# Linear attention with a cosine feed-forward layer: attention chunks of 128 steps split into two sub-chunks of 64 steps

## Chip, cores and metric

One core of one Trainium2 chip. The metric is the device time of one run in microseconds (us); lower is better. Engines: PE (TensorE, matmuls; PEld is its weight load), DVE (VectorE), ACT (ScalarE), POOL (GpSimd), SP (SyncE, which here only issues DMAs).

## The reference

4 batches, 8 heads, 768 steps, head size 48. All in float32.

```python
for t in range(S):                      # per batch and head; state is 48 x 48
    y[t]  = r[t] @ (state + outer(u * k[t], v[t]))
    state = w[t][:, None] * state + outer(k[t], v[t])
x = y as (4*768 tokens, 8*48 = 384)
h = x @ w_in                            # 384 -> 2048
out = (h * cos(h)) @ w_out              # 2048 -> 384
```

## The kernel before

**Attention.** Each batch's 768 steps are cut into 6 chunks of 128, so there are 24 chunks; two chunks (the same place of two batches) make a block, and there are 12 blocks. Blocks 0 and 6 hold first chunks (no state yet), blocks 5 and 11 last chunks (no state needed after). Heads come in 4 pairs, a pair's two heads at partitions 0 to 47 and 64 to 111. The steps of a chunk, by the letters of the plan:

- `decay` (L202): two scans on DVE make the running products of w inside the chunk and from its end; r is multiplied by the one (L220), k by the other (L221).
- `diag` (L223): the u-weighted diagonal, spread on POOL into the two score tiles `asb` (L239), one for each head of the pair.
- `t` (L264): 4 transposes of k on PE, copied to `kn`.
- `a` (L254): 8 score matmuls (4 pairs x 2 heads, 48 rows, 128 x 128 result); then two DVE copies under a mask (L261) put the scores above the diagonal into `asb`.
- `s` (L277), for a block: k-by-v products into `pst` (L286), added on DVE to the decayed state (L293).
- `o` (L306), for a block: own products, v by `asb`, 16 matmuls over 128 steps into two PSUM banks `py`.
- `d` (L246): the state times the whole chunk's decay, `dd`. `p` (L318), for a block: `dd` times r is added into `py` (L326), ACT copies both banks to `yf`, and DMAs spread `yf` into `xf` (L335 and L302): 6 DMAs for each chunk, half from SP, half from ACT.
- `x` (L337): `xf` is split in a high and a low part, `xT`.

An fp32 matmul leaves two records of PE in the trace, a transpose one.

**Feed-forward.** Each block of 256 tokens passes 8 units. `mm1` (L377 on, matmuls at L390) is 18 matmuls of 128 weights and 256 columns; the gate (L354 on: ACT, DVE, ACT, ACT, DVE, then the high part, then two POOL subtractions) makes h cos h; `mm2` (L396 on, matmuls at L404) is 12 matmuls with 384 columns, three units behind (`LAG`). So there are 96 of each.

**Order.** PE's order is written out by hand: `START` for the first blocks, while the weights are fetched and unpacked on ACT and DVE, and then `PLAN`, eight rows, one per unit of a block, each naming the attention steps that stand between `mm1` and `mm2` (the number after + is the chunk or block, counted from the running one). The other engines follow in the order that a scheduler gives from priorities; `tc.high_priority` moves an instruction forward in it. `NEEDS` and `att()` pull a step forward that another needs. `BUFS` has the buffers of each tile; `EARLY` and `LATER` say which engine does which step in the two phases. Attention uses three PSUM banks in turn (two while two blocks run side by side).

Of the kernel before, what the change touches and what calls it, by code (L numbers as in the profile page):

```python
# [44 lines left out]
EARLY = dict(rkt="v", cd="a", wsg="v", wadd="v", wm="a", whi0="a", whi1="a", ksh="a", gh="a", yf="a", xh="a", rzh0="p", rzh1="v", r3="v", k3="p", rk="v", ru="p", rf0="v", rf1="v", kn="a", dd="v", rd0="a", rd1="a", rz0="v", rz1="v", ks="v", g0="p", g1="p", x="v", wlo0="v", wlo1="v", qf="s", qt="s", qr="s", qv="s", qx0="s", qx1="s", qo="s")  # L45
LATER = dict(ksh="v", gh="v", yf="a", xh="v", rzh0="a", rzh1="a", r3="p", k3="v", rk="v", ru="v", rf0="v", rf1="v", kn="v", dd="p", rz0="v", rz1="v", ks="p", g0="p", g1="p", x="v", qf="s", qt="s", qr="s", qv="s", qx0="s", qx1="a", qo="s")
# [11 lines left out]
START = ["lv0 decay0 diag0 t0 load0 f load1 d0 a0 f f f diag1 w t1 decay2 o0 f w diag2 d1 load3 lv3 d2 diag3",  # L58
# [10 lines left out]
def rwkv_cos_ffn(ctx: ExitStack, tc: tile.TileContext, tr, tn, u, ut, wts, w, rkw, vst, us, xs, out):  # L69
# [44 lines left out]
    shrink = cst.tile([R, NP], F32, name="shrink")  # L114
# [66 lines left out]
    def att_load(j):  # L181
# [5 lines left out]
        a["r3"] = tt[:, 0:512].rearrange("p (a t) -> p a t", a=NP)  # L187
        a["k3"] = tt[:, 512:1024].rearrange("p (a t) -> p a t", a=NP)
# [54 lines left out]
    def rows(h):

        return slice(ROW * h, ROW * h + HD)

    def att_dstate(a):

        if a["c"] == 0:
            return  # L250
        a["dd"] = dd = buf("dd", [R, NP, HD], F32)
        E["dd"].tensor_tensor(out=dd, in0=states[a["b"]], in1=a["ee"][:, :, 0:1].to_broadcast([R, NP, HD]), op=ALU.mult)
# [424 lines left out]
```

## Time and profile before

| | |
|---|---|
| time, median of 3 runs | 577.27 us (576.62 to 577.53) |
| span of the profiled execution, first to last instruction | 575.5 us |
| PE busy | 526.2 us, 91% |
| PEld busy | 500.6 us, 87% |
| DVE busy | 422.8 us, 73% |
| ACT busy | 247.6 us, 43% |
| POOL busy | 239.4 us, 42% |
| in the chain that ended last: PE, DVE, DMA | 60%, 21%, 8% |

The profiled execution's span is 1.8 us under the median; no other time of that execution is given. Busy shares are averages over a start of about 157 us, in which weights are prepared, and a regular part after it.

### The profile page before, as it was taken

What the parts mean: (1) busy time and instruction counts of PE and PEld (TensorE: products, weight loads), DVE (VectorE), ACT (ScalarE), POOL (GpSimd) and SP (SyncE); (2) the same over time, 40 slices, a digit from 0 to 9 for tenths busy, and PEclk for the clock granted to TensorE, in tenths of its full rate; (3) what the DMA queues carried; (4) which work ended last, traced back from release to release, by engine and by line L of the source; (5) the groups of instructions that cost most, each with busy time, mean ns of one, the idle gap of its engine ahead of it and who ended that gap; (6) DMA issues with size and microseconds to landing.
All of it is one profiled execution on the core that took longest, in us unless ns stands there. A gap on an engine that the chain in (4) does not pass through costs nothing.

```text
span 575.5 us, 11251 instructions
## 1 busy us (share of the span) xinstructions
PE 526.2 (91%) x4444; PEld 500.6 (87%) x4444; DVE 422.8 (73%) x694; ACT 247.6 (43%) x420; POOL 239.4 (42%) x288
## 2 busy tenths in 40 slices
PE   2667699987999999999999999999999999999995
PEld 2556698986999999899999999999899999999994
DVE  6988999998886967856858857857858559835441
ACT  2336777673443442442442342342342534335441
POOL 2240437464534544532643634534534443323331
PEclk9998999998999999999999999999999999999998
DMA  8937583010526116026132025034033026210001
GB/s 231 271 114 255 181 281 110 2 56 27 159 104 168 40 35 188 12 59 177 49 115 71 4 94 142 1 105 130 1 108 100 1 100 223 91 29 1 28 1 33
DMA packets 22988, 56.12 MB, mean 98 GB/s; under 512 B 4240, under 2 KB 15120, under 8 KB 22928
## 3 DMA queue, kind: packets, MB, share of 16 engines
q1 hardware_dynamic: 20336, 53.55, 30.5%
q10 hardware_dynamic: 2592, 1.77, 1.2%
q8 instruction: 37, 0.61, 0.4%
q14 instruction: 23, 0.19, 0.1%
HBM read 45.87 MB, written 4.72 MB: 88 GB/s over the span
## 4 chain that ended last, share of the span: by engine, by line
PE 60%; DVE 21%; DMA 8%; issue 4%; ACT 4%; POOL 2%; ACTq 0%; SPq 0%; DVEq 0%; POOLq 0%
PE ph L390 26%; PE acc L404 24%; PE pa L259 3%; PE py L316 3%; DMA xf<-yf 3%; DMA tt<-tr 3%; DVE tt L216 2%; DVE h L172 2%; DVE ee L209 2%; DVE h L165 2%; DVE w L141 2%; PE py L326 2%; DVE rr L362 2%; DVE rr L359 1%; PE pst L286 1%
## 5 line engine op out<-in xcount | busy, mean ns | idle before, releaser
L141 POOL TENSOR_TENSOR gs<-rr,gs 128x256 fp32r<-128x256 f32 x192 | 162.8, 869 | 224.1 <-DVE gs L138 168.4
L390 PE MATMUL ph<-xT,w 128*128 128x256 f32 x1728 | 227.6, 287 | 13.5 <-DVE rr L362 4.9
L390 PEld LDWEIGHTS ph<-xT,w 128*128 128x128 f32 x1728 | 217.2, 192 | 18.9 <-issue 4.8
L404 PE MATMUL acc<-w,gs 128*128 128x384 f32 x1152 | 220.4, 339 | 4.1 <-DVE gs L138 2.8
L404 PEld LDWEIGHTS acc<-w,gs 128*128 128x128 f32 x1152 | 197.3, 189 | 9.7 <-DVE gs L138 4.0
L360 ACT ACTIVATE rr<-rr 128x512 f32<-128x512 f32 x96 | 60.7, 632 | 130.0 <-DVE rr L359 130.0
L358 ACT ACTIVATE rr<-ph 128x512 int32<-128x512 f32 x96 | 56.5, 588 | 114.3 <-PE ph L390 76.9
L362 DVE SCALAR_TENSOR_TENSOR rr<-rr,ph 128x512 f32<-128x512 f32 x96 | 65.5, 682 | 49.1 <-ACT rr L361 48.6
L359 DVE SCALAR_TENSOR_TENSOR rr<-rr,ph 128x512 f32<-128x512 int32 x96 | 65.2, 679 | 27.7 <-ACT rr L358 27.4
L361 ACT ACTIVATE rr<-rr 128x512 f32<-128x512 f32 x96 | 60.6, 631 | 2.4
L239 POOL TENSOR_SCALAR_AFFINE_SELECT asb<-cd 128x512 f32<-128x512 f32 x48 | 34.6, 743 | 33.3 <-PE py L316 17.5
L138 DVE CAST gs<-rr 128x512 fp32r<-128x512 f32 x80 | 37.6, 470 | 9.6 <-PE acc L404 9.2
L209 DVE TENSOR_TENSOR_SCAN ee<-tt,one_e 112x516 f32<-112x516 f32 x24 | 30.8, 1285 | 15.1 <-DMA tt<-tr 14.7
L220 POOL TENSOR_TENSOR tt<-tt 112x512 f32<-112x512 f32 x18 | 24.1, 1340 | 32.4 <-DVE tt L216 32.4
L259 PE MATMUL pa<-tt 48*128 48x128 f32 x384 | 32.6, 305 | 4.2 <-DVE tt L220 3.5
L259 PEld LDWEIGHTS pa<-tt 48*128 48x128 f32 x384 | 27.2, 204 | 10.4 <-issue 5.6
L261 DVE COPY_PREDICATED asb<-mask,pa 128x512 f32<-128x512 uint8 x48 | 33.5, 729 | 1.6 <-PE pa L259 1.6
L216 DVE TENSOR_TENSOR_SCAN tt<-tt,inj 112x516 f32<-112x516 f32 x24 | 33.1, 1378 | 0.1
L316 PE MATMUL py<-asb,v 128*64 128x128 f32 (+1 forms) x384 | 27.5, 302 | 2.1 <-DVE asb L261 2.1
L316 PEld LDWEIGHTS py<-asb,v 128*64 128x64 f32 (+1 forms) x384 | 23.8, 145 | 4.7 <-DVE asb L261 3.3
L138 ACT CAST w<-h 128x768 fp32r<-128x768 f32 x16 | 13.2, 828 | 23.4 <-DVE h L172 23.4
L227 PE MATMUL pc<-u_by_head,rkt 112*128 112x2 f32 x48 | 9.3, 316 | 13.3 <-DVE rkt L206 9.4
(68 smaller groups left out, 365.3 us busy)
## 6 DMA issues: line engine op xcount, KB each, us to landing
tt<-tr SPq DMA_DIRECT2D x24, 674.2 KB, 5.9
raw<-wts SPq DMA_DIRECT2D x16, 768.0 KB, 5.6
rk<-tn SPq DMA_DIRECT2D x18, 384.0 KB, 4.1
v<-tn SPq DMA_DIRECT2D x24, 192.0 KB, 4.5
out<-ob SPq DMA_DIRECT2D x24, 192.0 KB, 2.0
ww<-w SPq DMA_DIRECT2D x6, 768.0 KB, 4.3
xf<-yf SPq DMA_DIRECT2D x30, 72.0 KB, 2.4
xf<-yf ACTq DMA_DIRECT2D x18, 72.0 KB, 3.5
```

The lines of the kernel that those rows point to most:

```text
L138: (nc.scalar.copy if E[name] is nc.scalar else E[name].tensor_copy)(out=out, in_=in_)
L141: E[name].tensor_tensor(out=out, in0=full, in1=high.bitcast(F32), op=ALU.subtract)
L216: nc.vector.tensor_tensor_scan(out=wp[:, 0:W129], data0=wp[:, 0:W129], data1=inj.rearrange("p a t -> p (a t)"), initial=0.0, op0=ALU.mult, ...
L259: nc.tensor.matmul(out=pa[h][:, p], lhsT=a["k3"][rows(h), p], rhs=a["r3"][rows(h), p], start=True, stop=True)
L316: nc.tensor.matmul(out=py[SWAPPED[p]][ROW * o:ROW * o + m, n, p // 2], lhsT=a["v"][:, head_cols(p, h, m)], rhs=a["asb", h][:, p], start=n ...
L358: nc.scalar.activation(nn, ph, AF.Copy, scale=INV2PI / W_SCALE)
L359: nc.vector.scalar_tensor_tensor(out=rr, in0=nn, scalar=-2.0 * math.pi * W_SCALE, in1=ph, op0=ALU.mult, op1=ALU.add)
L360: nc.scalar.activation(rr, rr, AF.Sin, scale=0.5 / W_SCALE)
L361: nc.scalar.activation(rr, rr, AF.Square)
L362: nc.vector.scalar_tensor_tensor(out=rr, in0=rr, scalar=-0.5, in1=ph, op0=ALU.add, op1=ALU.mult)
L390: nc.tensor.matmul(out=ph[:, fi], lhsT=wgt[u * FU + fi][:, 0, a, kt * 128:(kt + 1) * 128], rhs=xT[:, b, kt], start=n == 0, stop=n == 3 * K ...
L404: nc.tensor.matmul(out=accs[i][j][:, :DM], lhsT=gs[:, a, fi, j * C:(j + 1) * C], rhs=wgt[u * FU + fi][:, 1, b], start=u == 0 and fi == 0 a ...
```

## The change

Each chunk is cut into two sub-chunks of 64 steps (q = 0, 1). The decay scans restart at each sub-chunk (8 instead of 4 stretches of the same total length). Scores, own products, state products and products with the past are made for each sub-chunk, with 64 rows or 64 columns, so that four matmuls address the four 64 x 64 quadrants of the array. The state is passed from the first sub-chunk to the second inside the block. Own products come in two visits, `o` and `b`, each with one sub-chunk of every pair; after each a small DVE copy (`settled`) reads the PSUM bank. Scores (`A`) and transposes (`T`) come once per block in the plan, no longer once per chunk. `xf` is one tile per block, and its DMAs are 6 per block. The diagonal tile is made by a POOL multiplication. `START`, `PLAN` and `PAIR` are new.

```diff
-BUFS = dict(... asb=4, ... kn=2, ee=2, dd=2, xf=6, ...)
+BUFS = dict(... asb=2, whole=6, sn=2, s0=2, ... kn=1, ee=2, dd=4, xf=2, ...)
-PLAN = ["t+2 t+3 mm1 mm2",
-        "a+2 mm2 mm1 decay+4",
-        "mm2 a+3 mm1 diag+4",
-        "mm1 o+1 mm2 diag+5 p+1 load+6 lv+6 load+7 lr+7 x+2",
-        "mm1 s+1 mm2 lv+7 x+3",
-        "mm1 mm2",
-        "mm1 mm2",
-        "mm1 d+4 d+5 mm2 decay+5 lr+6"]
+PLAN = ["T+1 mm2 mm1",
+        "mm1 A+1 mm2 decay+4",
+        "mm1 s+1 mm2 diag+4",
+        "mm1 o+1 mm2 decay+5",
+        "mm1 b+1 mm2 diag+5",
+        "p+1 mm1 mm2 load+6 lv+6 load+7 lr+7",
+        "mm2 mm1 x+2 lv+7",
+        "mm1 d+4 d+5 mm2 x+3 lr+6"]
...
+    def decayed(a, q, state):
+        w_all = a["whole"].rearrange("p (a q) -> p q a", q=2)[:, q].unsqueeze(2).to_broadcast([R, NP, HD])
+        a["dd", q] = dd = buf("dd", [R, NP, HD], F32)
+        (nc.vector if q and a["c"] == 0 else E["dd"]).tensor_tensor(out=dd, in0=state, in1=w_all, op=ALU.mult)
+    def att_scores(some):
...
+                for q in range(2):
+                    for h in range(2):
+                        nc.tensor.matmul(out=pa[h][subs(q), n, p], lhsT=a["k3"][rows(h), 2 * p + q],
+                                         rhs=a["r3"][rows(h), 2 * p + q], start=True, stop=True)
...
+                    nc.tensor.transpose(out=pt[h][:part * SUB, n, p, :HD], identity=ident[rows(h), rows(h)],
+                                        in_=a["k3"][rows(h), 2 * p:2 * p + part].rearrange("p q t -> p (q t)"))
...
+                    for q in range(2 if a["c"] < NCB - 1 else 1):
+                        nc.tensor.matmul(out=pst[q][ROW * h:ROW * h + m, n, p], lhsT=a["kn"][subs(q), n, head_cols(p, h, m)],
+                                         rhs=a["v"][subs(q), at:at + HD], start=True, stop=True)
...
+                    mid = buf("s0", [R, NP, HD], F32)
+                    nc.vector.tensor_tensor(out=mid, in0=pst[0][:R, n], in1=a["dd", 0], op=ALU.add)
+                decayed(a, 1, mid)
...
+    def att_own(i, second=0):
...
+            for pair in ((1, 0), (2, 3)) if second else ((0, 1), (3, 2)):
+                for p in pair:
+                    q = SWAPPED[p] ^ second
...
+                        nc.tensor.matmul(out=outs[i][SWAPPED[p]][ROW * o:ROW * o + m, n, p // 2, subs(q)],
+                                         lhsT=a["v"][subs(q), head_cols(p, h, m)], rhs=a["asb"][subs(q), h, n, p],
...
+        with tc.high_priority(offset=HP):
+            nc.vector.tensor_copy(out=settled[ROW:ROW + 1], in_=outs[i][SWAPPED[p]][ROW:ROW + 1, n, p // 2, subs(q)][:, 0:1])
...
+            for q in range(0 if a["c"] > 0 else 1, 2):
+                for p in (0, 1, 3, 2):
+                    for h in range(2):
+                        nc.tensor.matmul(out=py[SWAPPED[p]][rows(h ^ SWAPPED[p]), n, p // 2, subs(q)], lhsT=a["dd", q][rows(h), p],
+                                         rhs=a["r3"][rows(h), 2 * p + q], start=False, stop=True, skip_group_check=True)
```

## Rows read from the trace of the kernel before

**Rows 1.** The page: span, and busy time, share and instructions of each engine.

```profile
span 575.5 us, 11251 instructions
PE 526.2 (91%) x4444; PEld 500.6 (87%) x4444; DVE 422.8 (73%) x694; ACT 247.6 (43%) x420; POOL 239.4 (42%) x288
```

**Rows 2.** Busy time by stage: stretch, its length, busy time (and instructions) of PE, PEld, DVE, ACT, POOL, then the granted clock of PE, the DMA share and GB/s. The last one is one block of the plan.

```profile
0.00:40.00 40.00, 21.29 (x146) 18.80 (x148) 33.83 (x56) 13.74 (x22) 13.42 (x19) 1.00 0.74 195
40.00:80.00 40.00, 29.86 (x230) 27.72 (x228) 36.42 (x48) 25.75 (x40) 10.15 (x9) 0.91 0.70 237
80.00:120.00 40.00, 37.39 (x300) 35.43 (x298) 39.83 (x57) 29.61 (x49) 22.89 (x18) 1.00 0.28 88
120.00:157.00 37.00, 30.42 (x262) 28.09 (x262) 32.75 (x46) 17.85 (x32) 20.71 (x23) 0.95 0.29 84
157.00:290.34 133.34, 131.28 (x1149) 124.64 (x1147) 97.36 (x174) 50.93 (x90) 60.36 (x74) 1.00 0.31 93
417.47:459.11 41.64, 41.64 (x378) 40.07 (x377) 29.75 (x53) 16.07 (x30) 18.70 (x24) 1.00 0.24 72
```

**Rows 3.** The waits of PE from 157 us to the end: us in total, times, longest.

```profile
PE acc L404 <- DVE gs L138: 2.8, 5, 0.9
PE acc L404 <- POOL gs L141: 0.7, 2, 0.5
PE ph L390 <- DVE rr L362: 0.6, 1, 0.6
```

**Rows 4.** PE's timeline over one block of the plan (start in us, time to the modelled end of the last record, instruction, records). What a group costs is the distance from its start to the next one's.

```profile
417.47 1.16 PE L259 MATMUL pa<-tt 48*128 48x128 f32 x16
418.56 4.58 PE L390 MATMUL ph<-xT,w 128*128 128x256 f32 x36
423.07 1.96 PE L316 MATMUL py<-asb,v 128*64 128x128 f32 x32
424.96 2.36 PE L404 MATMUL acc<-w,gs 128*128 128x384 f32 x12
427.25 1.09 PE L326 MATMUL py<-tt,dd 48*48 48x128 f32 x32
428.27 1.13 PE L286 MATMUL pst<-v,kn 128*64 128x48 f32 x32
429.33 2.42 PE L390 MATMUL ph<-xT,w 128*128 128x256 f32 x18
431.59 2.25 PE L404 MATMUL acc<-w,gs 128*128 128x384 f32 x12
433.67 2.31 PE L390 MATMUL ph<-xT,w 128*128 128x256 f32 x18
435.82 2.25 PE L404 MATMUL acc<-w,gs 128*128 128x384 f32 x12
...
446.38 0.93 PE L268 MATMUL pt<-ident,tt 112*128 112x112 f32 x8
447.08 2.40 PE L390 MATMUL ph<-xT,w 128*128 128x256 f32 x18
...
459.11 1.16 PE L259 MATMUL pa<-tt 48*128 48x128 f32 x16
```

**Rows 5.** PE's timeline through one group of products with the past, cut at 341.66, 341.81 and 341.92 us (records started by then), and its last records.

```profile
341.63 0.33 PE L326 MATMUL py<-tt,dd 48*48 48x128 f32 x4
341.63 0.44 PE L326 MATMUL py<-tt,dd 48*48 48x128 f32 x8
341.63 0.55 PE L326 MATMUL py<-tt,dd 48*48 48x128 f32 x12
...
342.43 0.29 PE L326 MATMUL py<-tt,dd 48*48 48x128 f32 x4
```

**Rows 6.** Groups of instructions over the whole span, each shape apart: line, engine, operation, out<-in, shapes, count, then busy us and mean ns of one, then idle time before them.

```profile
L239 POOL TENSOR_SCALAR_AFFINE_SELECT asb<-cd 128x512 f32<-128x512 f32 x48 | 34.6, 743 | 33.3 <-PE py L316 17.5 <-ACT cd L138 8.9 <-DVE cd L235 6.1
L261 DVE COPY_PREDICATED asb<-mask,pa 128x512 f32<-128x512 uint8 x48 | 33.5, 729 | 1.6 <-PE pa L259 1.6
L220 POOL TENSOR_TENSOR tt<-tt 112x512 f32<-112x512 f32 x18 | 24.1, 1340 | 32.4 <-DVE tt L216 32.4
L252 POOL TENSOR_TENSOR dd<-sn,ee 112x192 f32<-112x192 f32 x16 | 7.9, 516 | 15.3 <-DVE sn L293 15.3
L138 DVE COPY kn<-pt 128x384 f32<-128x384 f32 x14 | 7.6, 549 | 0.7 <-PE pt L268 0.7
L293 DVE TENSOR_TENSOR sn<-pst,dd 112x192 f32<-112x192 f32 x16 | 4.9, 348 | 4.3 <-PE pst L286 4.3
L138 ACT COPY kn<-pt 128x384 f32<-128x384 f32 x6 | 2.8, 465 | 0.0
```

**Rows 7.** ACT's timeline after the past products of a block; ACTq is its queue issuing DMAs.

```profile
342.77 1.07 ACT L138 COPY yf<-py 112x512 f32<-112x512 f32 x2 [2.01 <-PE py L326]
343.87 0.53 ACTq L335 DMA_DIRECT2D xf<-yf  x1
...
350.37 0.60 ACT L358 ACTIVATE rr<-ph 128x512 int32<-128x512 f32 x1 [6.53 <-PE ph L390]
```

**Rows 8.** DVE's timeline in the block of rows 4: the last write of the next block's input, and a gate cast among its longest.

```profile
440.24 0.59 DVE L141 TENSOR_TENSOR xT<-xf,xT 128x384 fp32r<-128x384 f32 x1
...
446.30 1.05 DVE L138 CAST gs<-rr 128x512 fp32r<-128x512 f32 x1
```

More of the change, by code (lines that the diff above doesn't have):

```diff
@@ L243, in rows @@
[L243 to L252, printed above, removed]
-    def att_scores(a):
-        pa = [bank("a", [C, NP, C], "pa") for h in range(2)]
-        for p in range(NP):
-            for h in range(2):
-                nc.tensor.matmul(out=pa[h][:, p], lhsT=a["k3"][rows(h), p], rhs=a["r3"][rows(h), p], start=True, stop=True)
-        for h in range(2):
-            nc.vector.copy_predicated(a["asb", h], mask, pa[h])
@@ L263, in att_transpose @@
-    def att_transpose(a):
-        if a["c"] == NCB - 1:
-            return
-        pt = bank("a", [C, NP, 2, ROW], "pt")
-        for p in range(NP):
-            nc.tensor.transpose(out=pt[:, p].rearrange("t h d -> t (h d)")[:, :R], in_=a["k3"][:, p], identity=ident[:R, :R])
-        a["kn"] = kn = buf("kn", [C, DM], F32)
-        copy("kn", kn.rearrange("t (a h d) -> t a h d", h=2, d=HD), pt[:, :, :, :HD])
+        n = a["j"] % BLK
+        if n == 0:
+            a["asb"] = buf("asb", [C, 2, BLK, NP, SUB], F32)
+        else:
+            a["asb"] = atts[a["j"] - n]["asb"]
@@ new lines, in att_dstate @@
+    def att_dstate(a):
+        if a["c"] > 0:
+            decayed(a, 0, states[a["b"]])
+    def att_scores(some):
+        pa = [bank("a", [C, BLK, NP, SUB], "pa") for h in range(2)]
+        for a in some:
+            n = a["j"] % BLK
+            for p in range(NP):
+                for q in range(2):
+                    for h in range(2):
+                        nc.tensor.matmul(out=pa[h][subs(q), n, p], lhsT=a["k3"][rows(h), 2 * p + q],
+                                         rhs=a["r3"][rows(h), 2 * p + q], start=True, stop=True)
+        at = slice(some[0]["j"] % BLK, n + 1)
+        for h in range(2):
+            nc.vector.copy_predicated(some[0]["asb"][:, h, at], mask.unsqueeze(1).to_broadcast([C, len(some), NP, SUB]), pa[h][:, at])
@@ new lines, in att_transpose @@
+    def att_transpose(some):
+        pt = [bank("a", [C, BLK, NP, SUB], "pt") for h in range(2)]
+        part = 2 if some[0]["c"] < NCB - 1 else 1
+        for a in some:
+            n = a["j"] % BLK
+            a["kn"] = buf("kn", [C, BLK, DM], F32) if n == 0 else atts[a["j"] - n]["kn"]
+            for p in range(NP):
+                for h in range(2):
+                    nc.tensor.transpose(out=pt[h][:part * SUB, n, p, :HD], identity=ident[rows(h), rows(h)],
+                                        in_=a["k3"][rows(h), 2 * p:2 * p + part].rearrange("p q t -> p (q t)"))
+        at = slice(some[0]["j"] % BLK, n + 1)
+        kn = some[0]["kn"].rearrange("t n (a h d) -> t n a h d", h=2, d=HD)
+        for h in range(2):
+            copy("kn", kn[:part * SUB, at, :, h], pt[h][:part * SUB, at, :, :HD])
@@ L277, in att_state @@
     def att_state(i):
-        two = [a for a in (atts[i * BLK + n] for n in range(BLK)) if a["c"] < NCB - 1]
-        pst = bank("a", [C, BLK, NP, HD], "pst") if two else None
+        two = [atts[i * BLK + n] for n in range(BLK)]
+        pst = [bank("a", [C, BLK, NP, HD], "pst") for q in range(2)]
         for n, a in enumerate(two):
@@ L330, in att_past @@
         copy("yf", yf[:, :, 1:3], py[1][:R])
+        xf = buf("xf", [128, BLK, KT, C], F32)
         for n in range(BLK):
-            xf = atts[i * BLK + n]["xf"] = buf("xf", [128, KT, C], F32)
-            for h in range(2):
-                part = yf[rows(h), n]
-                E["qx%d" % h].dma_start(out=xf[h * HD:(h + 1) * HD], in_=part[:, 0:3])
-                spread(xf, part[:, 3], h)
+            atts[i * BLK + n]["xf"] = xf[:, n]
+        for h in range(2):
+            E["qx%d" % h].dma_start(out=xf[h * HD:(h + 1) * HD], in_=yf[rows(h), :, 0:3])
+            spread(xf, yf[rows(h), :, 3], h)
     def att_x(a):
@@ L437, in att @@
         for m in ("decay" if n == "diag" and j < BY_PE else NEEDS.get(n, "")).split():
-            for c in (range(j * BLK, (j + 1) * BLK) if whole and m not in "osp" else (j,)):
+            for c in (range(j * BLK, (j + 1) * BLK) if whole and m not in "obspTA" else (j,)):
                 att(c, m)
@@ L455, in att @@
             att_load(j)
+        elif n in "TA":
+            both = [j * BLK + m for m in range(BLK) if (j * BLK + m, n.lower()) not in seen]
+            seen.update((c, n.lower()) for c in both)
+            if both:
+                steps[n]([atts[c] for c in both])
         else:
```

139 lines of the change are left out of this document (72 added, 67 removed), and 8 rows, old and new, of the table START.

## The prediction

> **What bounds the kernel now.** First the page: PE is busy 91% of the span [rows 1]. A share says little over stages, so next the stages [rows 2]. Until 157 us PE idles 38 us (157 less 21.3, 29.9, 37.4 and 30.4), and DVE is busy 33.8, 36.4 and 39.8 of three times 40 us: that start is set by DVE's unpacking of weights and the chains around it. From 157 us on PE is the bound: 131.3 of 133.3 us, then 41.64 of 41.64 us in one block of the plan, with DVE at 29.8, POOL at 18.7 and ACT at 16.1. Third, PE's waits in that part [rows 3]: 4.1 us in all, 3.5 of them for gate outputs that DVE and POOL deliver late. So a microsecond less of PE work in a block is a microsecond of time, from 157 us on; before that it mostly is not.
>
> Fourth, what a block of PE consists of [rows 4]. One mm2 takes 2.08 us (431.59 to 433.67), one mm1 2.15; eight of each make 33.9. Attention groups: scores 1.09 twice, own products 1.89, past 1.02, state 1.06, transposes 0.70, together 6.85. The remaining 0.9 of 41.64 lies at the edges: mm2 after the own products takes 2.29 instead of 2.08, about 0.1 on entering and 0.1 on leaving a visit whose matmuls do not fill the array. Four such visits at 0.21 and a cheap one (the transposes) make 0.9. **Attention on PE is 7.8 us of a block.**
>
> **What a quadrant costs.** The past products already use four quadrants (48 rows, 48 columns). Their records start in fours: 4, 8 and 12 records by 341.66, 341.81 and 341.92, the last four at 342.43 [rows 5], so 8 quartets at 0.109 to 0.114 us; with 0.15 at the end that is 1.02 [rows 4]. I write a group as sets x cadence + 0.15. State: 16 pairs in 1.06, so 0.057 a pair, with 48 columns and weights 64 wide; scores: 8 pairs in 1.09, 0.117, with 128 and 128. The own products, 16 pairs of 128 columns in 1.89, give 0.109 again.
>
> After the change a set is four matmuls with 64 (or 48) columns and weights 48 to 64 wide. Bounds of its cadence: below, half the past's quartet, 0.055; above, the past's quartet unchanged, 0.109, if halving the columns buys nothing. I take 0.058, nearest the state row: it is the only row with weights 64 wide and few columns.
>
> PE, one block after: scores 64 records, 16 sets, 1.08; state the same, 1.08; past 64 records, 1.08; own products two visits of 8 sets, 0.61 each; transposes 16, in pairs over the rows, 8 sets, 0.61 if they go at the state's cadence (bounds 0.5, and 1.09 at the scores' cadence, whose weights are 128 wide too). Sum 5.07. Visits: T, A, s, o, b, p, six at 0.21, 1.26, since the past and state products no longer share one. Together 6.33 against 7.78: **1.45 less**.
>
> From 157 us on nine blocks remain (3 to 11). Six regular ones: -8.7. Block 6 has no past before (6.76) and half of one after (5.86): -0.9. Blocks 5 and 11 have neither transposes nor state products before (5.93) but half of both after (5.75): -0.2 each. **PE term: -10.0 us**.
>
> **The other engines.** DVE, per block: two mask copies of 512 go (2 x 729 ns), the kn copies move to ACT (2 x 549 ns), two more state additions come (2 x 348 ns) and two `settled` copies of one element at 0.2 us (no row has one; bounds nothing and the 348 ns of an addition): -1.5 us of 29.8 [rows 2, 6]. ACT gains two copies near 465 ns [rows 6], but after the past products it issues three DMAs for the block rather than six: today its next gate step starts at 350.37, 6.5 us after the copies at 342.77 to 343.84, behind those issues [rows 7]. I take 3 us of that as freed, half (bounds 0 and 6.5). SP's issues halve too, with the same bytes. POOL: four selects (743 ns) become two multiplications (1340 ns by the r product), two more `dd` (516 ns): +0.7 of 18.7, hidden by 22 us of idle time. With less on DVE and ACT the gate outputs come earlier; of the 4.1 us of waits [rows 3] I take half away: -2 (bounds 0 and -4.1).
>
> **New waits.** `settled` stands on DVE between an own visit and the next writer of `py`. `b` follows `o` after mm2 and mm1, 4.2 us; `p` follows `b` after a single mm2, 2.08 us. Ahead of `settled` DVE may be inside an operation of 1.05 us or so [rows 8] and then needs 0.2: covered once, not with two such in front. Behind it in DVE's order wait gate steps, three units (12.7 us) ahead of their mm2. I take one block in three losing 0.7: +2 to +3, taken as +2 (bounds 0, and 1.1 in each of 12 blocks, +13). The state chain (sum, second `dd` on POOL 0.52, past) has two visits, two mm2 and two mm1 before `p`: hidden.
>
> The next block's input: the past start at 427.25, the last write of xT ends at 440.83 [rows 8], its mm1 is at 447.08 [rows 4], 6.2 us to spare. After, `p` has only three mm1, four mm2 and T before that mm1, 16.8 us instead of 19.8; the 3 us from fewer DMA issues give it back. Loads of the next chunk move two rows later in the plan, still four rows (17 us) ahead of their scan. Both cost nothing while that cover lasts.
>
> **The start.** Three blocks of attention shrink there, 4.4 us of PE at most, half of which I count where PE is near its bound (37.4 of 40 us [rows 2]). DVE there changes by: 12 mask copies half as long (-2.8), four state additions (+1.4), six more `dd` (about 516 to 615 ns each on it, +3), `settled` (+1): near +2.5. The first block gains a chain (state, second `dd`, past) before its x. Net 0, bounds -6 and +5; this is the least certain term, since the whole order of the start is new.
>
> **Sum.** Against the profiled execution: 575.5 - 10 - 2 + 2 + 0 = 565.5 of span. The median stands 1.8 us above that span; I add it: **567.3 us**.
>
> **Rivals.**
> 1. *Halving the columns buys nothing*: sets keep 0.109, because what spaces the records is their issue and not their columns. For: no group of rows 4 has records closer than 0.027 us on average (past 0.87 us for 32); the changed kernel has some 1640 more of them. Against: within a quartet four records start inside 0.03 us [rows 5]. Then a block costs 3 x 1.89 + 2 x 1.02 + 0.61 + 1.26 = 9.58, +1.8; nine blocks +18: **595 us**. It decides from a cadence of 0.081 on, where 64 sets eat the gain.
>
> A rule on issue bears on this. The Trainium skill, "TensorE: Matmul & The Clock Gate", section "Wait — 56ns, not 53.3ns?", says that starts of matmuls never come closer than about 25 ns, however small they are. By that figure a set of four takes 0.100 us, a regular block 9.0 us, and the time would be about 591, an estimate. The quartets of [rows 5] break it between quadrants, but not as a mean over a group.
>
> 2. *`settled` eats the gain*: DVE, near 70% busy, has two operations ahead of it in most blocks and `p` waits about 1.1 us in each: 12 x 1.1 = 13 instead of 2: **578 us**. For: DVE is in order and late in these rows already [rows 3]. Against: it loses 1.5 us of work in a block, and the copy is moved forward by priority.
> 3. *Only pairs overlap*: the quadrants do not run four at a time when both halves of a chunk share rows. Cadence 0.058 for two, 10.1 a block: near 598 us. The past products speak against it.
> 4. *The start gains as well*: shorter first chains let the first mm1 begin earlier, -6, and the waits vanish, -4: **557 us**. For: PE idles 38 us there. Against: DVE, which fills that stage, does not get less work.
>
> **Chances.** The forecast, 560 to 572: 0.52. Rival 4: 0.13. Rival 2 with all that ends between 572 and 582: 0.18. Rivals 1 and 3: 0.17. The range 554 to 582 holds the first three but for tails, 0.8. A measurement of this kernel tells about 0.2% (1.2 us). Faster takes forecast, rival 4 and the lower half of rival 2's band: 0.74; within 0.2%: 0.05; slower 0.21.
>
> **What would show it.** Right: score, state and past groups of 64 records at 1.0 to 1.15 us, own visits near 0.6, a regular block near 40.2 us, PE records about 6080. Wrong: quartets near 0.1 us; waits of the past or second own products for DVE above 0.5 us per block; PE waiting for xT at a block's first mm1; or the last weight's unpacking, and with it the regular part, starting several us later than 157.

## The result and the profile after

The changed kernel takes 585.87 us (median; 582.12 to 586.86) against 577.4 for the kernel before in the same runs: ratio 1.0148, 95% interval 1.0106 to 1.0189. It is slower by 1.5%. The forecast was 567.3, range 554 to 582, faster; the time lies outside the range and on the other side. The profiled execution took 586.22 us, its span is 584.5. In the table of experiments a median is over all executions and a ratio over the undisturbed ones alone; of e2's four executions two were disturbed, the profiled one among them, so its marks stand in brackets.

The page after (answers to [rows 1]): PE has 11 us less work, and yet the span is 9.0 us longer. So PE idles 20 us more.

```profile
span 584.5 us, 14459 instructions
PE 514.9 (88%) x6084; PEld 489.4 (84%) x6084; DVE 415.9 (71%) x716; ACT 258.5 (44%) x445; POOL 241.7 (41%) x280
```

To divide those 9.0 us I use two marks: the start of the 17th mm1 (the third block's first, where the regular part begins) and of the 96th, the last. Before they stand at 157.4 and 557.6 us, after at 164.4 and 566.3. **Start +7.0, regular part 401.9 against 400.2, so +1.7, end +0.3.** The regular part was to lose 10.

Busy time by stage after, columns as in [rows 2]. In the last line, one block, PE idles 1.4 of 41.6 us (the stretch opens inside a wait of 2.40 us); the block of [rows 2] has no idle time.

```profile
0.00:40.00 40.00, 17.20 (x282) 14.98 (x285) 34.43 (x61) 14.17 (x24) 9.39 (x14) 1.00 0.72 233
40.00:80.00 40.00, 27.21 (x369) 24.33 (x367) 37.70 (x55) 23.49 (x36) 13.30 (x9) 0.87 0.62 188
120.00:164.00 44.00, 36.03 (x434) 32.52 (x434) 36.27 (x61) 16.95 (x32) 24.17 (x23) 0.92 0.28 83
417.00:458.60 41.60, 40.18 (x512) 38.59 (x512) 25.60 (x50) 16.87 (x30) 19.50 (x24) 1.00 0.23 63
```

The waits of PE from 168 us on (answers to [rows 3]; total, times, longest). The two waits for gate outputs of before (3.5 us) are nearly gone. In their place stands one that [rows 3] has at 0.6 us: mm1 waits until DVE has read a PSUM bank `ph` of an earlier mm1 (its last reader is L403). One more wait, 0.7 us for `xT`, lies between the first mark and 168 us: 14.1 us in all from mark to mark, 4.1 before.

```profile
PE ph L431 <- DVE rr L403: 11.1, 6, 2.4
PE pst L313 <- DVE asb L281: 1.3, 1, 1.3
PE py L348 <- DVE s L320: 0.6, 1, 0.6
PE acc L445 <- POOL gs L155: 0.4, 1, 0.4
```

PE's timeline over one block (answers to [rows 4]). Every group costs what was forecast: scores 294.39 to 295.48, 1.09; state 1.06 (of 32 records: half the others are missing); own products 0.62 twice; past 1.04; transposes 0.63. The loss is in the mm1 at 248.53 and 290.58, each the second of two mm1 that follow one another (row 0 of PLAN ends with mm1, row 1 begins with it): 1.76 and 1.88 us of idle time in front of them. The first takes 2.29 us, the second 3.81 (the last section shows its clock), and another one, at 460.60, takes 3.38, and the scores behind it 1.49 for 1.09.

```profile
248.53 2.36 PE L431 MATMUL ph<-xT,w 128*128 128x256 f32 x18 [1.76 <-DVE rr L403]
250.82 1.16 PE L277 MATMUL pa<-tt 48*64 48x64 f32 x64
...
256.31 1.13 PE L313 MATMUL pst<-v,kn 64*64 64x48 f32 x32
257.37 2.35 PE L445 MATMUL acc<-w,gs 128*128 128x384 f32 x12
...
261.76 0.69 PE L348 MATMUL py<-asb,v 64*64 64x64 f32 x32
262.38 2.35 PE L445 MATMUL acc<-w,gs 128*128 128x384 f32 x12
...
266.78 0.69 PE L348 MATMUL py<-asb,v 64*64 64x64 f32 x32
267.39 2.35 PE L445 MATMUL acc<-w,gs 128*128 128x384 f32 x12
269.67 1.11 PE L367 MATMUL py<-tt,dd 48*48 48x64 f32 x64
270.71 2.38 PE L431 MATMUL ph<-xT,w 128*128 128x256 f32 x18
...
283.59 0.70 PE L291 MATMUL pt<-ident,tt 48*128 48x48 f32 x16
284.22 2.36 PE L445 MATMUL acc<-w,gs 128*128 128x384 f32 x12
286.42 2.28 PE L431 MATMUL ph<-xT,w 128*128 128x256 f32 x18
290.58 3.88 PE L431 MATMUL ph<-xT,w 128*128 128x256 f32 x18 [1.88 <-DVE rr L403]
294.39 1.16 PE L277 MATMUL pa<-tt 48*64 48x64 f32 x64
295.48 0.79 PE L445 MATMUL acc<-w,gs 128*128 128x384 f32 x3
...
460.60 3.44 PE L431 MATMUL ph<-xT,w 128*128 128x256 f32 x18 [2.14 <-DVE rr L403]
463.98 1.56 PE L277 MATMUL pa<-tt 48*64 48x64 f32 x64
465.47 2.35 PE L445 MATMUL acc<-w,gs 128*128 128x384 f32 x12
```

Why L403 is late stands in DVE's timeline ahead of 290.58. ACT's L399 (273.57, 0.60 long) is done with the mm1 of 270.71 at 274.17. L400, DVE's next step for it, starts at 278.30: in front of it in DVE's order is a scan (L223) that waits 2.76 us for a load. From there on the delay is handed down. The next L399 ends at 280.79; its L400 comes at 286.10, behind two more scans; its L403, at 289.77, frees the bank for which PE has waited since 288.70.

```profile
277.15 1.24 DVE L223 TENSOR_TENSOR_SCAN ee<-tt,one_e 112x520 f32<-112x520 f32 x1 [2.76 <-DMA tt<-tr]
278.30 0.66 DVE L400 SCALAR_TENSOR_TENSOR rr<-rr,ph 128x512 f32<-128x512 int32 x1
...
282.88 1.67 DVE L223 TENSOR_TENSOR_SCAN ee<-tt,one_e 112x520 f32<-112x520 f32 x1
284.48 1.71 DVE L230 TENSOR_TENSOR_SCAN tt<-tt,inj 112x520 f32<-112x520 f32 x1
286.10 0.66 DVE L400 SCALAR_TENSOR_TENSOR rr<-rr,ph 128x512 f32<-128x512 int32 x1
...
288.62 1.23 DVE L230 TENSOR_TENSOR_SCAN tt<-tt,inj 112x520 f32<-112x520 f32 x1
289.77 0.66 DVE L403 SCALAR_TENSOR_TENSOR rr<-rr,ph 128x512 f32<-128x512 f32 x1
```

The load itself (from issue to landing, median, from 164 us on) takes 7.1 us; before, from 157 us on, it took 5.4. Now both of a block's loads stand behind `p`, beside the six DMAs of x. The load for the scan at 277.15 was issued at 270.43, 6.7 us ahead of it: DVE had come to that scan at 274.4 and stood there until the load landed. (Before, after, and the issue on SP's queue.)

```profile
tt<-tr SPq DMA_DIRECT2D x14, 674.2 KB, 5.4
tt<-tr SPq DMA_DIRECT2D x14, 675.9 KB, 7.1
270.43 0.33 SPq L200 DMA_DIRECT2D tt<-tr  x1
```

### The profile page after: what moved, and what is told of

Read it like the earlier page. It is cut to its first block, busy times and chain, and to the rows that moved or that the text cites. A ratio compares the mean times of both kernels' runs of the same rounds, so it can differ in the third digit from the quotient of the medians.

```text
span 584.5 us, 14459 instructions
## 1 busy us (share of the span) xinstructions
PE 514.9 (88%) x6084; PEld 489.4 (84%) x6084; DVE 415.9 (71%) x716; ACT 258.5 (44%) x445; POOL 241.7 (41%) x280
## 4 chain that ended last, share of the span: by engine, by line
PE 47%; DVE 34%; DMA 10%; issue 4%; ACT 2%; SPq 1%; POOL 1%; DVEq 0%; ACTq 0%
PE acc L445 21%; PE ph L431 19%; DMA xf<-yf 5%; DVE tt L230 5%; DVE ee L223 4%; DMA tt<-tr 3%; DVE rr L403 3%; DVE w L155 2%; DVE rr L400 2%; DVE h L179 2%; PE py L348 2%; DVE h L186 2%; PE py L367 2%; DVE shrink L226 2%; DVE h L178 1%
## 5 line engine op out<-in xcount | busy, mean ns | idle before, releaser
L400 DVE SCALAR_TENSOR_TENSOR rr<-rr,ph 128x512 f32<-128x512 int32 x96 | 65.1, 678 | 49.0 <-ACT rr L399 49.0
L403 DVE SCALAR_TENSOR_TENSOR rr<-rr,ph 128x512 f32<-128x512 f32 x96 | 65.4, 682 | 41.0 <-ACT rr L402 39.9
L399 ACT ACTIVATE rr<-ph 128x512 int32<-128x512 f32 x96 | 56.8, 591 | 82.0 <-PE ph L431 68.6
L223 DVE TENSOR_TENSOR_SCAN ee<-tt,one_e 112x520 f32<-112x520 f32 x24 | 35.3, 1472 | 24.9 <-DMA tt<-tr 24.9
L152 DVE CAST gs<-rr 128x512 fp32r<-128x512 f32 x79 | 33.8, 428 | 6.5 <-PE acc L445 5.4
L255 POOL TENSOR_TENSOR asb<-cd,diag 128x512 f32<-128x512 f32 x24 | 27.6, 1151 | 23.8 <-ACT cd L152 12.2
L230 DVE TENSOR_TENSOR_SCAN tt<-tt,inj 112x520 f32<-112x520 f32 x24 | 33.5, 1395 | 0.2
L348 PE MATMUL py<-asb,v 64*64 64x64 f32 (+1 forms) x768 | 18.6, 232 | 5.5 <-DVE settled L354 2.1
L348 PEld LDWEIGHTS py<-asb,v 64*64 64x64 f32 (+1 forms) x768 | 14.8, 135 | 9.5 <-DVE settled L354 2.5
L245 DVE TENSOR_TENSOR rk<-rk 128x384 f32<-128x384 f32 x18 | 12.9, 717 | 12.2 <-DMA rk<-tn 12.1
L277 PE MATMUL pa<-tt 48*64 48x64 f32 x768 | 17.7, 242 | 3.5 <-DVE tt L233 1.9
L277 PEld LDWEIGHTS pa<-tt 48*64 48x64 f32 x768 | 15.3, 152 | 6.0 <-ACT xT L152 2.0
L291 PE MATMUL pt<-ident,tt 48*128 48x48 f32 (+1 forms) x192 | 10.6, 239 | 9.5 <-POOL tt L234 9.4
```

Source lines behind the costliest of these rows:

```text
L152: (nc.scalar.copy if E[name] is nc.scalar else E[name].tensor_copy)(out=out, in_=in_)
L230: nc.vector.tensor_tensor_scan(out=wp[:, 0:W65], data0=wp[:, 0:W65], data1=inj.rearrange("p a t -> p (a t)"), initial=0.0, op0=ALU.mult, o ...
L348: nc.tensor.matmul(out=outs[i][SWAPPED[p]][ROW * o:ROW * o + m, n, p // 2, subs(q)], lhsT=a["v"][subs(q), head_cols(p, h, m)], rhs=a["asb" ...
L399: nc.scalar.activation(nn, ph, AF.Copy, scale=INV2PI / W_SCALE)
L400: nc.vector.scalar_tensor_tensor(out=rr, in0=nn, scalar=-2.0 * math.pi * W_SCALE, in1=ph, op0=ALU.mult, op1=ALU.add)
L403: nc.vector.scalar_tensor_tensor(out=rr, in0=rr, scalar=-0.5, in1=ph, op0=ALU.add, op1=ALU.mult)
```

## The experiments

Each was timed against the kernel before on the same chip. "17th" and "part" are the two marks: start of the 17th mm1, and from there to the 96th, both from the one profiled execution.

| run | median, us | ratio to before [95%] | 17th, us | part, us |
|---|---|---|---|---|
| before | 575.4 to 577.4 | 1 | 157.4 | 400.2 |
| after | 585.87 | 1.0148 [1.0106, 1.0189] | 164.4 | 401.9 |
| e1_alternate | 574.73 | 0.9981 [0.9964, 0.9999] | 165.2 | 391.8 |
| e2_start_decay5 | 593.27 | 1.0199 [1.0153, 1.0245] | (168.6) | (409.1) |
| e3_four_banks | 590.93 | 1.0265 [1.0233, 1.0297] | 162.9 | 406.5 |
| e4_w_first | 573.09 | 0.9946 [0.9926, 0.9967] | 164.0 | 391.4 |
| e5_both | 568.23 | 0.9858 [0.9838, 0.9878] | 163.6 | 384.9 |
| e6_before_w_first | 568.18 | 0.9848 [0.9824, 0.9871] | 155.1 | 395.2 |
| e7_old_start_order | 573.42 | 0.9955 [0.9924, 0.9985] | 171.0 | 382.4 |
| e8_before_merged_x | 573.96 | 0.9968 [0.9946, 0.9990] | 155.6 | 397.4 |
| e9_block1_chain | 574.2 | 0.9958 [0.9929, 0.9987] | 170.8 | 383.2 |
| e10_first_scores | 563.85 | 0.9778 [0.9743, 0.9813] | 160.3 | 383.3 |
| e11_high_priority | 568.26 | 0.9856 [0.9827, 0.9886] | 163.2 | 384.9 |
| e12_chain_and_scores | 571.14 | 0.9910 [0.9879, 0.9941] | 168.0 | 383.1 |
| e13_mm1_sooner | 566.41 | 0.9817 [0.9800, 0.9833] | 163.2 | 383.7 |
| e14_loads_sooner | 563.65 | 0.9793 [0.9756, 0.9829] | 160.5 | 382.7 |
| e15_mm1_and_loads | 566.09 | 0.9816 [0.9800, 0.9833] | 162.3 | 384.3 |
| e16_state_sooner | 566.44 | 0.9830 [0.9804, 0.9856] | 164.6 | 383.9 |
| e17_chain_close | 568.15 | 0.9879 [0.9835, 0.9923] | 165.2 | 382.3 |
| e18_diag_to_pool | 570.45 | 0.9923 [0.9901, 0.9945] | 161.8 | 388.1 |

**The regular part: e1 to e6.** Theory: the second of two adjacent mm1 comes too early for DVE, which is held up by scans waiting for loads. Rivals: too few `ph` banks; the start's order.

e1, the mm1 taken apart:

```diff
-PLAN = ["T+1 mm2 mm1", ... "mm2 mm1 x+2 lv+7",
+PLAN = ["T+1 mm1 mm2", ... "mm1 mm2 x+2 lv+7",
```

> The changed kernel with two rows of PLAN altered: row 0 mm1 before mm2, row 6 mm1 before mm2, so that no two mm1 stand side by side in the regular part. Theory A (the regular part lost its 10 us of matmul gain because mm1 pairs leave too little time for the gate to give back one of three ph banks): the waits of mm1 for DVE's last gate step (11.1 us after 168 us) fall below 3 us, the granted clock drops inside the regular part go, and the time falls from 585.9 to about 574. Rival B (DVE is late because its scans stand ahead of the gate and wait for loads, whatever the order of the matmuls): the waits stay above 8 us, perhaps under another name (mm2 for gate outputs), and the time stays within 2 us of 585.9.

e3, a bank taken from attention and given to mm1:

```diff
-BANKS = dict(a=("a0", "a1", "a2"), h=("h0", "h1", "h2"))
+BANKS = dict(a=("a0", "a1"), h=("h0", "h1", "h2", "a2"))
```

> The changed kernel with four PSUM banks in turn for mm1 outputs and two for attention in the regular part (before three and three). Theory A (mm1 waits for a bank, because three do not cover the gate's delay): the waits of mm1 for DVE's last gate step fall under 2 us; attention visits wait up to 0.5 us each for the copies of the visit before; the time falls by 6 to 10 us, to 576 to 580. Rival B (DVE late in itself): the waits reappear as mm2 waiting for gate outputs and the time falls by less than 3 us.

e4, the load of a chunk in two DMAs, the part that the scans read first:

```diff
-        E["qt"].dma_start(out=tt, in_=tr[g])
+        E["qt"].dma_start(out=tt[:, 1024:], in_=tr[g][:, 1024:])
+        E["qt"].dma_start(out=tt[:, 0:1024], in_=tr[g][:, 0:1024])
```

> The changed kernel with each chunk's load cut in two DMAs, the decay factors (521 of 1545 columns) first, r and k after. Theory B (DVE's scan, queued ahead of the gate step, waits for the whole load: 24.9 us of DVE idle time before the scans): that idle time falls under 12 us, the waits of mm1 for DVE's last gate step fall by half, and the time falls by 4 to 6 us. Theory A (only the order of the matmuls): DVE idles less, but the time stays within 2 us of 585.9.

e5 is e1 and e4 together, e6 is e4's edit made in the kernel before.

> The changed kernel with both the alternating PLAN rows and the decay factors loaded first. If the two edits take away the same wait (mm1 for a ph bank, because the gate step on DVE is late), they do not add up: about 572 to 574 us. If they cure different things they add up: about 562 us.

> The kernel before with each chunk's load cut in two, decay factors first, nothing else. If the early scan matters only where the changed PLAN puts it against the mm1 pairs, the kernel before gains little: 573 to 577 us (some of its 4.1 us of waits). If a faster scan is worth as much in any order, it gains 10 us or more, to 565.

The waits of PE from 168 us on: the largest of e3, the largest of e4, and both of e5:

```profile
PE pa L277 <- ACT kn L152: 9.9, 10, 2.1
```

```profile
PE ph L432 <- DVE rr L404: 5.2, 6, 1.2
```

```profile
PE py L349 <- DVE s L321: 0.5, 1, 0.5
PE pst L314 <- DVE asb L282: 0.4, 2, 0.2
```

e1 removes the wait on `ph` and 10.1 us of the part; e4, which touches no order of PE, takes 10.5; its time falls by about 12 us, where 4 to 6 were expected. So the loss has two conditions, the pair and the late load, and either one removed takes 10 of the 17.0 us that go with both. DVE's idle time in front of the scans, for the load, says the same (168 to 570 us): 22.7 us after, 21.1 in e1, 8.3 in e4, 3.9 in e5. In e1 the scans wait as long as ever, and most of it no longer reaches PE; 4.6 us of other waits are left there, of the scores and the state products above all. e3 ends outside both expectations. The `ph` wait is gone, and the scores wait instead for ACT to copy the transposes out of the two banks left (9.9 us); ahead of such a copy ACT itself has waited for the late gate step of DVE, as in the line below. Since e3 gives mm1 a bank by taking one from attention, it does not show what a bank more would be worth; its waits sum to 12.8 us, 13.4 after.

```profile
207.79 0.63 ACT L401 ACTIVATE rr<-rr 128x512 f32<-128x512 f32 x1 [2.50 <-DVE rr L400]
```

e6 is the surprise: the scans' wait on the load costs the kernel before as well, 5.0 us of its part and 8 us of its time. DVE's idle time for the load in front of the scans falls there from 14.2 to 1.0 us. So the net worth of the change is to be read between e5 and e6, both without these waits: **384.9 against 395.2, 10.3 us less** from the 17th mm1 on, which a start longer by 8.5 us and an end longer by 1.2 eat up (568.23 and 568.18). A regular block takes about 40.0 us in e5 and 41.6 in e6, some 1.6 less for the 1.45 forecast.

e8 is the kernel before with `xf` as one tile per block and 6 DMAs for it, not 12.

```diff
-BUFS = dict(... xf=6, ...)
+BUFS = dict(... xf=3, ...)
...
-                E["qx%d" % h].dma_start(out=xf[h * HD:(h + 1) * HD], in_=part[:, 0:3])
...
+            E["qx%d" % h].dma_start(out=xf[h * HD:(h + 1) * HD], in_=yf[rows(h), :, 0:3])
```

> The kernel before with one part of the change alone: xf as one tile per block, 6 DMAs per block in place of 12. The forecast counted 3 us of ACT time freed per block and 2 us less waiting in all: 575 us or 1 to 3 us under the kernel before. Rival: the merged transfers land later (5.0 and 6.3 us in the changed kernel, 2.4 and 3.5 before), what ACT gains is lost again, and the time stays within 1.2 us.

It gives 2.8 us of the part in the profiled execution, and PE's waits there fall from 4.1 to 2.2 us. By the ratio the whole gain is 0.3% (0.1 to 0.5%), about 1.8 us.

**The start: e2, e7, e9 to e18.** After, block 0's first scores start at 20.92 us, 12.61 before; its first mm1 at 49.2 and 41.0. In PE's hand order the second chunk's transposes, which wait for POOL, stand ahead of those scores:

```profile
18.05 0.66 PE L291 MATMUL pt<-ident,tt 48*128 48x48 f32 x8 [8.84 <-POOL tt L234]
...
20.92 1.51 PE L277 MATMUL pa<-tt 48*64 48x64 f32 x32
```

e10, on e5:

```diff
-START = ["... load1 f f f t1 diag1 a0 a1 ...",
+START = ["... load1 a0 f f f t1 diag1 a1 ...",
```

> Edit against e5_both: in START the scores of the first chunk stand ahead of the transposes of the second one, which wait for POOL (8.8 us of PE's time at 18 us). Theory (block 0's chain sets the first mm1): scores at 13 instead of 21 us, first mm1 near 42 instead of 47, 17th mm1 1 to 5 us earlier, time 562 to 567. Rival (DVE's unpacking of weights sets the start): the first mm1 comes earlier or not, the 17th mm1 stays within 2 us of 163.6, time 567 to 569.

The scores start at 11.55, the first mm1 at 45.1 (46.8 in e5), the 12th at 110.0 (116.9), the 17th 3.3 us earlier, and the part is 1.6 us shorter besides. With e14, which does not differ from it beyond noise, this is the fastest kernel of the study: 2.2% under the kernel before and, by the two ratios, 0.7% under e6, which is the kernel before with the same loads.

```profile
11.55 1.35 PE L278 MATMUL pa<-tt 48*64 48x64 f32 x32 [1.14 <-ACT kn L152]
16.57 0.66 PE L292 MATMUL pt<-ident,tt 48*128 48x48 f32 x8 [3.66 <-POOL tt L235]
```

The other 5.2 us (160.3 against 155.1 in e6) withstood every other attempt. Up to the 12th mm1 e10 is ahead of e6, 110.0 against 113.4; the loss lies between the 12th and the 17th, in block 2: 50.3 us against 41.7. PE idles 11.0 us of that stretch in e10 and 5.1 in e6, and its granted clock is 0.94 in e10 (in two pieces of the stretch at the 1.2 GHz level) and 1.00 in e6. (Columns as in [rows 2]; e10, then e6.)

```profile
109.98:160.32 50.34, 39.38 (x460) 35.95 (x460) 44.62 (x74) 20.66 (x38) 28.36 (x25) 0.94 0.29 85
113.41:155.09 41.68, 36.60 (x320) 33.85 (x319) 37.76 (x55) 21.23 (x38) 25.18 (x25) 1.00 0.27 78
```

e2, on after, brings block 2's scans and visits forward:

```diff
-  "... diag4 lv4 mm1 ...", "mm1 w diag5 decay5 ... a4 mm1 w t5 ... a5 mm1 s2 mm1 w o2 ...", "b2 p2 ..."
+  "... diag4 lv4 decay5 mm1 ...", "mm1 w diag5 a4 t5 ... a5 mm2 mm1 w s2 ... o2 ... b2 ... p2 mm2", "mm1 mm2 ..."
```

> The changed kernel with only the last two rows of START altered: the decay of chunk 5 right after the diagonal of chunk 4, and the six visits of block 2 placed closer together among the same feed-forward units. Theory (the start is 8.4 us longer because block 2's attention, a longer chain of six dependent visits, is finished too late): the 17th mm1 moves from 165.9 to about 158 to 160 us and the time falls by 5 to 8 us, to 578 to 581. Rival (the start is set by DVE's total work): the 17th mm1 moves by less than 2 us and the time by less than 2.

e7 (on e5) writes START and PAIR after those of before, a row of it below; e9 writes block 1's visits without an mm1 between them; e11 raises the priority of the small DVE steps; e12 is e9 and e10.

```diff
+  "a2 x0 f lv2 mm1 x1 t2 w decay3 t3 a3 s1 o1 f b1 mm1 p1 x2 x3 d3 load4 mm2 ...",   (e7)
-  "... t3 a3 mm1 f s1 mm1 f b1 w o1 load4 mm2 w mm1 f p1 w f w mm1 x2 z",
+  "... t3 a3 s1 o1 b1 p1 mm1 f mm1 f w load4 mm2 w mm1 f w f w mm1 x2 z",      (e9)
-HP = 50
+HP = 400                                                                        (e11)
```

> The version with both edits, and a START in the order of the kernel before: its PAIR, first scores ahead of the second transposes, and o, b and p of each block next to each other. Theory (the new START and PAIR cost the 7 us: the 17th mm1 at 164 to 165 us against 157.4 before, because PE waits for weights and for late chains): 17th mm1 at 156 to 160 and the time 6 us or so under the version with both edits. Rival (the longer chain of the sub-chunks costs it in any order): 17th mm1 stays above 163 and the time within 2 us.

> Edit against e5_both: in START the visits s1 o1 b1 p1 of block 1 stand in a row behind a3, with no mm1, mm2 or weight fetch between them. Theory (the start is late because block 1's chain of visits is drawn out: its past ends at 65 us where it ended at 56 before, so its first mm1 stands at 83 instead of 72): the past ends near 57, the first mm1 of block 1 comes 4 to 8 us earlier, the 17th mm1 near 158 instead of 163.6, time near 563. Rival (DVE's work and its order set the start, not the chain): the past comes earlier all the same but the 17th mm1 stays within 2 us of 163.6, time 567 to 570.

> Edit against e5_both: HP, by which the state additions, settled and the write-back are moved forward in the scheduler's order, 400 instead of 50. Theory (the chain's small DVE operations wait in DVE's queue behind long ones): the past of blocks 1 and 2 comes 2 us or more earlier each, 17th mm1 2 to 5 us earlier, time 562 to 566. Rival (they are not late; the chain is long because of where its visits stand in PE's order): same within 1 us, 567 to 569.

> Both edits of e9_block1_chain and e10_first_scores. Theory (chains set the start): the gains add, 17th mm1 near 156 to 158, time 559 to 563. Rival (DVE sets it): as e5_both, 567 to 570.

The theory of the drawn-out chain fell. e2 is 2.0% slower than the kernel before, no better than after. In e9 block 1's past starts at 58.6 instead of 63.7, but the first mm1, now behind it, at 60.5 instead of 46.8: PE waits 0.6 to 2.6 us for DVE ahead of nearly every visit, and the mm1 between them had filled that time. e12, e9 and e10 together, ends at 571.14, where the theory had 559 to 563. e7 is no better, 171.0. e11 changes nothing.

e13 to e18 go after block 2, on e10:

```diff
-  lr6 mm2 mm2 mm2 a4 mm1 w t5 w load6 d4 d5 mm2 a5 mm1 s2 mm1 w o2 w w f lv6 mm2", "b2 p2 mm1 mm2 ...
+  lr6 mm2 mm2 a4 mm1 mm2 w t5 ...                                              (e13)
+  lr6 load6 load7 mm2 mm2 mm2 a4 ...                                           (e14)
+  ... mm2 s2 a5 mm1 mm1 w o2 ...                                               (e16)
+  ... mm2 s2 a5 mm1 w o2 w w f lv6 mm1 b2 mm2 p2", "mm1 mm2 ...                (e17)
-LATER = dict(..., rk="v", ru="v", ...)
+LATER = dict(..., rk="p", ru="p", ...)                                         (e18)
```

> Edit against e10_first_scores: in START row 4 the third of three mm2 in a row goes behind the next mm1 ('mm2 mm2 a4 mm1 mm2' for 'mm2 mm2 mm2 a4 mm1'). Theory (PE's written order starves the gates here: PE waits 3 us for gate outputs in the three mm2 while ACT waits 6.9 us for the next mm1): block 2's scores and the next mm1 come 2 to 4 us earlier, 17th mm1 near 157 to 158 instead of 160.3, time 560 to 562. Rival (DVE, busy without a gap from 110 to 135 us, decides): 17th mm1 stays within 1 us of 160.3, time 563 to 565.

> Edit against e10_first_scores: in START the loads of chunks 6 and 7 stand at the beginning of row 4 (issued near 112 us, while the DMA engines idle) instead of behind the second transposes and in the plan. Theory (the diagonals and scans of block 3, waiting in DVE's queue for loads issued late, hold the gate's DVE steps: 4.4 us of ACT waiting for DVE at 148 to 153 us and 4.0 us of PE waiting for ACT at 153 to 157): PE's wait before the 17th mm1 falls under 2 us, 17th mm1 at 156 to 158, time 559 to 562. Rival (what stands before it on PE decides): within 1 us of 160.3, 563 to 565.

> Both edits of e13_mm1_sooner and e14_loads_sooner. Theory: the gains add, 17th mm1 at 153 to 156, near the 155.1 of the kernel before with the same load form, time 556 to 559. Rival (DVE's work decides): 159 to 161, 562 to 565.

> Edit against e10_first_scores: in START row 4 the state products of block 2 go ahead of the second chunk's scores (s2 a5 mm1 mm1 for a5 mm1 s2 mm1). They need no scores, and the state sums, the second dd and the own products wait for them. Theory (what is left of the late start is block 2's chain scores, state, sums, own, settled, own, settled, past, 14.7 us from 130.2 to 144.9 in e10, where it is 9 us in the kernel before): past of block 2 near 142 instead of 144.9, 17th mm1 near 158 instead of 160.3, time 560 to 562. Rival (the chain is not what sets it; DVE is busy without a gap there): 17th mm1 within 1 us of 160.3, 563 to 565.

> As e16_state_sooner, and block 2's two visits of own products and its past follow with one mm1 or mm2 between each (o2 mm1 b2 mm2 p2). Theory: past of block 2 near 139 to 141, 17th mm1 at 155 to 157, time 557 to 560. Rival: settled and the masks are waited for in front of PE, the past comes sooner but mm1 and mm2 are pushed back by as much; 17th mm1 at 159 to 162, 562 to 566.

> Edit against e10_first_scores: in the later phase the two multiplications of the diagonal (rk) are made by POOL, not DVE. From 121 to 162 us they fill about 10 us of DVE and stop it another 3 us for their load. Theory (DVE's queue sets the stretch from 110 to 160 us: every step of block 2's longer chain passes through it): 17th mm1 at 154 to 158 instead of 160.3, time 557 to 562; in the regular part no change, since PE waits for nothing there. Rival (the chain's visits in PE's order set it, or the gates on POOL come late in turn): 17th mm1 within 1 us of 160.3 or later, 563 to 568.

None moved the 17th mm1 forward; in e13, e15, e16 and e17 it comes 2.0 to 4.9 us later. Each reordering of PE met another wait for DVE: e13 3.68 us of state products for the masked copy, e16 5.6 us of scores for the state sums. In e18 DVE is busy 26.4 of the 41 us from 121 us on, 35.2 in e10, and the mark still stands at 161.8. So less work for DVE alone does not help: POOL, busy 30.3 us there for 19.7, now keeps DVE waiting for 2.76 us, and the part is 4.8 us longer, where no change was expected. What all of them share is the last wait ahead of the mark, an mm2 waiting 2.9 to 4.7 us for a gate (0.7 in e6), and in front of that gate DVE standing still. In e10, e14, e16, e17 and e18 it stands for a load of the block after, 2.5 to 4.3 us (e10 below); in e13 and e15 for POOL's multiplication of the diagonal, 2.61 us, with no load or only 0.87 us of one:

```profile
150.33 0.56 DVE L246 TENSOR_TENSOR rk<-rk 128x384 f32<-128x384 f32 x1 [2.73 <-DMA rk<-tn]
150.92 0.56 DVE L247 TENSOR_TENSOR rk<-rk,u_sb 128x384 f32<-128x384 f32 x1
151.40 1.23 DVE L224 TENSOR_TENSOR_SCAN ee<-tt,one_e 112x520 f32<-112x520 f32 x1
152.66 0.69 DVE L401 SCALAR_TENSOR_TENSOR rr<-rr,ph 128x512 f32<-128x512 int32 x1
```

e14 moved the `tt` loads, not this one, and no run gave `rk` more than its two buffers. That this load makes the 5 us is not shown, and e13, which has no such load wait and reaches the mark later still, speaks against it; e18, where the scan waits 3.85 us for `tt` at the same place, speaks for its kind. The cause of the 5 us stays open: more waiting of PE in block 2, and the lower clock with it, is what the traces show.

## Why the prediction was wrong, step by step

**The quadrants: right.** Sets at 0.058 us were forecast and every group came within 0.04 us of the time that this gave. The PE term was -10.0; measured between e5 and e6, -10.3, and PE's waits in the two parts differ by 0.3 us only (0.9 and 1.2). Rival 1 falls with it: 64 score records take 1.09 us, 17 ns apart. The rule behind it, about 25 ns between starts at the least (the Trainium skill, "TensorE: Matmul & The Clock Gate", section "Wait — 56ns, not 53.3ns?"), is thus contradicted here as a mean over a group, when the records go to four quadrants. Rival 3 falls too.

**Relief of the gate waits, -2: right in size, drowned.** Fewer DMAs for x alone give -2.8 in the part and about -1.8 in all, by the ratio (e8). In the changed kernel the waits for gate outputs did shrink, from 3.5 to 0.4 us, while the waits on `ph` came up.

On the smaller terms: the `settled` copy takes 156 ns for the 0.2 us assumed, POOL's multiplication 1049 ns for 1340; ACT's next gate step comes 2.8 us after the start of the `yf` copies where it came 7.6 after [rows 7], so 4.8 us are freed for the 3 taken. Over the blocks it comes 2.7 to 3.2 us after them where it came 5.2 to 7.8. x is done at 282.86 for the mm1 at 286.42: 3.6 us to spare, not 6.2, but enough. (Groups by shape from 168 us on, then ACT's timeline.)

```profile
L255 POOL TENSOR_TENSOR asb<-cd,diag 128x512 f32<-128x512 f32 x14 | 14.7, 1049 | 7.1 <-DVE cd L248 4.7 <-PE py L348 2.4
L354 DVE COPY settled<-py 1x1 f32<-1x1 f32 x18 | 2.8, 156 | 0.6
```

```profile
270.82 1.07 ACT L152 COPY yf<-py 112x512 f32<-112x512 f32 x2 [1.23 <-PE py L367]
...
273.57 0.60 ACT L399 ACTIVATE rr<-ph 128x512 int32<-128x512 f32 x1 [1.68 <-PE ph L431]
```

**`settled`, +2: not there.** From 168 us on no wait for it shows, the copies take 156 ns each; the start has 4.4 us of them. Rival 2, the story for "slower", was the wrong story.

**The step that failed: "Loads of the next chunk move two rows later in the plan ... Both cost nothing while that cover lasts."** The cover of 17 us was counted in rows of PLAN, which is PE's order. DVE's order comes from the scheduler, and there the scan stands far ahead of its row: 6.7 us behind the issue of its load (270.43 and 277.15), where such a load takes 7.1 us to land (median). So the cover was not there, and I did not look at what stands behind the scan in DVE's queue. It was not there in the kernel before either, where DVE idles 14.2 us for these loads. The load's landing went from 5.4 to 7.1 us, the scans waited 22.7 us, and gate steps behind them waited too. What the later place of the loads in PLAN costs by itself is not shown: e4 leaves them there, and no run moves them back. I also read PLAN for the attention steps alone: that rows 0 and 1, and 6 and 7, put mm1 next to mm1, twice a block where the plan before has one such pair (418.56 in [rows 4], x36), stood in the diff. The balance of the part closes within about 1 us: PE -10.3; waits from 4.1 to 14.1, +10.0; matmuls at the lower clock, two mm1 of 3.81 and 3.38 for 2.29 and scores of 1.49 for 1.09, +3.0. That makes +2.7, measured +1.7. My terms for old and new waits were 0 net, and the clock had no term.

**The start, net 0 (-6 to +5): +7.0.** It was called the least certain term and its bounds were still too narrow. Between e5 and e6 the start differs by 8.5 us, in two pieces: 3.3 us for scores written behind transposes that wait for POOL, which START showed; 5.2 us in block 2, whose cause stays open. DVE's added work was estimated at +2.5 us. To 160 us it is busy 146.6 in e10, 144.4 in e6, +2.2; but up to each kernel's own 17th mm1 it is 147.0 and 139.6, +7.4, so the agreement is luck of where one stops. An item was off as well: twelve mask copies half as long, written as -2.8, would be -4.4 by [rows 6], and they measured 435 ns for 718 in the start, -3.4.

## What to carry to other kernels

When work becomes cheaper on the engine that sets the pace, read the new written order for two like steps in a row, and ask of each in-order engine beside it what stands behind an instruction that waits for a load: that queue, not the busy share, decides whether the gain arrives. Where a transfer feeds the head of such a queue, send the part that is read first in a DMA of its own; here it was worth 1.5% in the kernel before, unchanged otherwise. An edit's worth shows only against a control that has the same repairs: e5 against before says -1.4%, against e6 nothing.

## What was not expected of the hardware

A short stall can cost more than its length. After the wait of 1.88 us at 288.70 the granted clock is 0.55 of full speed through the mm1 that follows, the 1.2 GHz level for most of it, and that mm1 takes 3.81 us; the mm1 before the wait runs at 1.00. Of the six such waits two were followed by it (1.88 and 2.14 us) and four were not (1.38, 1.53, 1.76 and 2.40), so the wait's length alone does not tell. In e1, e4 and e6, whose waits in the part are 1.2 us or less each, the clock never falls there. Columns as in [rows 2].

```profile
286.42:288.70 2.28, 2.28 (x19) 2.07 (x18) 2.28 (x7) 1.75 (x3) 1.04 (x1) 1.00 0.00 0
290.58:294.39 3.81, 3.81 (x18) 3.66 (x18) 2.92 (x6) 2.40 (x5) 2.64 (x4) 0.55 0.00 0
```

And smaller DMAs landed sooner here: the load as two DMAs of 448 and 228 KB lands in 5.0 and 3.8 us (median, e4), as one of 676 KB in 7.1. Sooner is not always better: the DMAs of x, merged for two chunks in e8, land in 4.3 to 5.1 us where they took 2.7 to 3.5, and yet e8 gained.
